# Front of a fused attention and squared-ReLU kernel: q of chunks 2 and 3 loaded ahead of the weights and multiplied while chunks 0 and 1 are normalised

## The chip, the cores and the metric

The kernel runs on one core of a Trainium2 chip. The core has five engines with an instruction queue each: PE (TensorE, matrix products into PSUM), DVE (VectorE, elementwise work), ACT (ScalarE, activations, copies and scalings), POOL (GpSimd) and SP (SyncE, which here only issues transfers). ACT and POOL issue transfers too. The metric is device time in microseconds (us); of the kernel before there are three runs, of 921.12, 923.35 and 923.43 us, with a median of 923.35.

## The reference

```python
kv  = einsum('bhsd,bhse->bhde', k, v)          # 8 batches, 8 heads, 576 rows, 64 columns
o   = einsum('bhsd,bhde->bhse', q, kv)
rms = sqrt(mean(o * o, axis=-1) + 1e-6)
x   = (o / rms * g_norm)                        # then (B,H,S,D) -> (B*S, H*D): 4608 x 512
h   = x @ w_in                                  # 512 -> 2048
g   = s * maximum(h, 0)**2 + b
out = g @ w_out                                 # 2048 -> 512
```

q, k, v and g_norm are float32. w_in and w_out come as float64 and are turned into float32 on the chip.

## The kernel before

The 4608 rows of x are cut into chunks of 128 rows, counted from 0; four chunks make a unit of 512 rows. Each unit goes through attention, then through the first matrix product with ReLU and squaring, then through the second. While PE multiplies one unit, the attention of the next is woven in. Only unit 0 has nothing in front of it: its four chunks, 0 to 3 (called 1 to 4 in the wording of the change), are worked off by a straight list of calls at the end of the kernel, from line 1272 on. Everything below is about this front.

The order is written out by hand. The kernel uses a manual schedule, so each engine gets its instructions in the order of the calls; the framework only adds the semaphore waits. A call such as `product` puts instructions on several engines at once, so moving it moves work in several queues.

Attention of a chunk `c` has these steps (`attention`, line 414):

- `turn` (L431): four PE transposes of q into a PSUM bank.
- `take` (L436 on DVE, L438 on ACT): copy of the turned q to SBUF (tile `qT`).
- `product`: the product with the block-diagonal kv matrices (`bd_kv`) into a PSUM bank, then the square on ACT (L456) and the sum of squares on DVE (L458). Chunks 0 and 1 use four 128x128 matmuls (L91), chunks 2 and 3 sixteen that are 32 wide (L447).
- `norm`: root on ACT (L462), reciprocal and scaling on DVE (L464, L466) into the tile `xn`.
- `turn_x`: the turn of `xn` into `xT`. Chunks 0 and 1 go through PE (L484), and ACT copies them out of PSUM scaled by g_norm (L486). Chunks 2 and 3 are transposed by DVE (L490), and ACT scales them in place for both at once (`scale_x`, L501).

The weights come in tiles of 1 MB, as pairs of 32-bit words, into a ring of three raw buffers (`w_raw`). `send_w` issues the next load on SP. A tile is made float32 by four calls: `hi` (L225) and `lo` (L230) on ACT prepare the upper and lower word, `shift` (L235) and `plus` (L245) on DVE put them together; `plus` also sends the next load. Each may be called for half a tile. Tile 0 is `wa` of step 0, tile 1 is `wb` of step 0, tile 2 is `wa` of step 1, and so on.

The first product of unit 0 is cut into 16 slots (`mm1_plain`, line 660). Each multiplies one weight tile with 256 rows, in 8 matmuls (the trace records each as two, so as 16), and puts its ReLU on ACT (L673) and its squaring on DVE (L674) at the place where the slot is called:

- slot 0: tile 0 with chunks 0 and 1, into an `x` bank
- slot 1: tile 1 with chunks 0 and 1, into a `y` bank
- slot 2: tile 0 with chunks 2 and 3
- slot 3: tile 1 with chunks 2 and 3; slots 4 to 15 go on with tiles 2 to 7.

Within a slot the matmuls run over four quarters of the 512 columns of x, so the second half of a weight tile is needed only after half of them.

The transfers of the front are issued on two queues, SP and ACT. A transfer waits for an earlier one to land when it takes over its semaphore. In the list, q of chunks 0 and 1 is loaded first, then weight tile 0, then q of 2 and 3, then tiles 1 and 2. `warm(n)` puts n matmuls of no use (2n in the trace) in the queue, which keep PE busy.

Of the kernel before, what the change touches and what calls it, by code (L numbers as in the profile page):

```python
# [16 lines left out]
def kernel(  # L17
# [113 lines left out]
    def load_q(c, queues=(nc.sync, nc.sync), rest_on=nc.gpsimd):  # L131

        t = qp.tile([P, 2 * DM], FP32, name="q_sb", tag="q")
        q_tile[c] = t
        pieces = []
        for i in range(2):
            if c + i < R:
                q_in[c + i] = t[:, i * DM : i * DM + DM].rearrange("p (h d) -> p h d", h=H)  # L140
        for s, queue in enumerate(queues):
            for i in range(2):
                if c + i < R:
                    b, j, _ = parts(c + i)[s]
                    queue.dma_start(
                        out=q_in[c + i][s * HB : s * HB + HB],
                        in_=q[b].rearrange("h (p j) d -> p j h d", j=R)[:, j],
                    )
        for i in range(2):
            if c + i < R:  # L150
                continue
            w = 4 * i
            for b, j, n in parts(c + i):
                if pieces and pieces[-1][1] == b and pieces[-1][2] + pieces[-1][3] == j:
                    pieces[-1][3] += n
                else:
                    pieces.append([w, b, j, n])
                w += n
            q_in[c + i] = t.rearrange("p (a w) -> p a w", a=NP)[:, :, i * P : i * P + P]
            if c + i == R:  # L160
                q_in[R] = t[:, DM:].rearrange("p (a w) -> p a w", a=NP)
        rest = []
        for w, b, j, n in pieces:
            src = q[b].rearrange("h (t j) d -> h t j d", j=JC)
            to = t.rearrange("p (a w d) -> p a w d", a=NP, d=32)
            if c < R:
                to, w = t[:, DM:].rearrange("p (a w d) -> p a w d", a=NP, d=32), 0
            for h in range(H):
                for a in range(2):
                    rows = slice(32 * (2 * (h % 2) + a), 32 * (2 * (h % 2) + a) + 32)  # L170
                    rest.append(
                        partial(
                            rest_on.dma_start,
                            out=to[rows, h // 2, w : w + n, :],
                            in_=src[h, :, j : j + n, a * 32 : a * 32 + 32],
                        )
                    )
        return rest
# [183 lines left out]
    def warm(n):  # L362

        ps = ps_f.tile([P, 2, TB], FP32, name="warm_ps", tag="z", bufs=1)
        for _ in range(n):
            matmul(ps[:, 0, :P], ident, ident, True, True)
# [35 lines left out]
    def half_of(name, c):  # L402

        if c % 2 == 0:
            two_of[name] = attp.tile([P, 2 * DM], FP32, name=name, tag=name)
        t = two_of[name]
        if name == "qT":
            return t.rearrange("p (a x) -> p a x", a=NP)[:, :, c % 2 * P : c % 2 * P + P]
        return t[:, c % 2 * DM : c % 2 * DM + DM].rearrange("p (h d) -> p h d", h=H)

    def small(name, n, i=""):
        return attp.tile([P, n], FP32, name=name, tag=f"{name}{i}")

    def attention(c):

        st = {}  # L420

        def turn():
            st["qT"] = half_of("qT", c)
            if c in (0, 2):
                ps = ps_a.tile([P, NP, P], FP32, name="qT_ps", tag="x")
            elif c == 3:
                ps = bank_of("q", "z", 1).rearrange("p b (m n) -> p (b m) n", m=2)
            else:
                ps = ps_t.tile([P, NP, P], FP32, name="qT_ps", tag="t")
            for p in range(NP):  # L430
                nc.tensor.transpose(ps[:, p, :], q_in[c][:, 2 * p : 2 * p + 2, :], ident)  # L431
            st["q_ps"] = ps

        def take():
            if c != 1:
                nc.vector.tensor_copy(out=st["qT"], in_=st["q_ps"])  # L436
            else:
                nc.scalar.copy(st["qT"], st["q_ps"])  # L438

        def product():  # L440
            ps = bank_of("att", "xy"[c % 2]).rearrange("p b (m n) -> p (b m) n", m=2)
            if c < 2:
                for p in range(NP):
                    matmul(ps[:, p, :], st["qT"][:, p, :], bd_kv[0][:, p, :], True, True)
            for w in range(4 if c >= 2 else 0):
                for p in range(NP):
                    nc.tensor.matmul(  # L447
                        ps[32 * p : 32 * p + 32, w, :],
                        lhsT=st["qT"][:, p, 32 * w : 32 * w + 32],
                        rhs=bd_kv[0][:, p, :],  # L450
                        start=True,
                        stop=True,
                    )
            st["x"] = ps.rearrange("p c (l d) -> p (c l) d", l=2)
            st["xn"] = half_of("xn", c)
            nc.scalar.activation(st["xn"], st["x"], AF.Square)  # L456
            st["ss"] = small("ss", H, c % 2)
            nc.vector.reduce_sum(st["ss"], st["xn"], axis=mybir.AxisListType.X)  # L458

        def norm():  # L460
            rms = small("rms", H, c % 2)
            nc.scalar.activation(rms, st["ss"], AF.Sqrt, bias=eps_col, scale=1.0 / D)  # L462
            inv = small("inv", H, c % 2)
            nc.vector.reciprocal(inv, rms)  # L464
            shape = (P, H, KC, D // KC)
            nc.vector.tensor_tensor(  # L466
                out=st["xn"].rearrange("p h d -> p (h d)").rearrange(
                    "p (c h e) -> p h c e", c=KC, h=H
                ),
                in0=st["x"].rearrange("p h (c e) -> p h c e", c=KC),  # L470
                in1=inv.unsqueeze(2).unsqueeze(3).to_broadcast(shape),
                op=ALU.mult,
            )

        def turn_x():
            u, j = divmod(c, 4)
            if j == 0:
                xT[u] = xp.tile([P, KC, 2 * TB], FP32, name="xT", tag="xT")
            to = xT[u][:, :, j * P : j * P + P]
            if c < 2:  # L480
                ps = ps_t.tile([P, KC, P], FP32, name="xT_ps", tag="t")
                xn = st["xn"].rearrange("p h d -> p (h d)")
                for i in range(KC):
                    nc.tensor.transpose(ps[:, i, :], xn[:, i * P : i * P + P], ident)  # L484
                for i in range(KC):
                    nc.scalar.activation(  # L486
                        to[:, i], ps[:, i], AF.Copy, scale=g_col[:, i : i + 1]
                    )
                return
            nc.vector.transpose(  # L490
                out=to, in_=st["xn"].rearrange("p h d -> p (h d)").rearrange("p (c x) -> p c x", c=KC)
            )
            if j % 2 == 1:
                scale_x(u, j - 1)

        return turn, product, norm, turn_x, take

    def scale_x(u, j):
        to = xT[u][:, :, j * P : j * P + 2 * P]
# [136 lines left out]
    def bank_of(key, tag, bufs=2):  # L636
        bank[key] = ps_f.tile([P, 2, TB], FP32, name=f"{tag}_ps", tag=tag, bufs=bufs)
        return bank[key]
# [598 lines left out]
    def send_w():  # L1237
        if sent[0] < len(blocks):
            load_w(blocks[sent[0]])
            sent[0] += 1  # L1240
# [9 lines left out]
    def hi(n, h=None):  # L1250
        fold_hi(blocks[n], h)

    def lo(n, h=None):
        round_lo(blocks[n], h)

    def shift(n, h=None):
        shift_hi(blocks[n], place(n), h)
# [16 lines left out]
    for i in range(2):  # L1274
        load_kv(0, i, kv0p, two, tag="kv")
    load_q(0, two)
    send_w()
    load_q(2, two[::-1])
    for _ in range(2):
        send_w()  # L1280
    kv_product(0)
    kv0p.release()
    gp = ctx.enter_context(tc.tile_pool(name="gp", bufs=NS // 2))


    turn, product, norm, turn_x, take = zip(*(attention(c) for c in range(4)))
    slots0 = [slot for s in range(NS) for slot in mm1_plain(s)]
    turn[0]()
    turn[1]()
# [1 line left out]
    take[1]()  # L1291
    product[0]()
    product[1]()
    warm(7)
    norm[0]()
    hi(0, 0)
    norm[1]()
    shift(0, 0)
    hi(0, 1)
    lo(0, 0)  # L1300
    plus(0, 0)
    turn_x[0]()
    turn_x[1]()
    turn[2]()
    turn[3]()
    lo(0, 1)
    take[2]()
    take[3]()
    shift(0, 1)
    product[2]()  # L1310
    plus(0, 1)
    hi(1)
    product[3]()
    shift(1)
    lo(1)
    plus(1)
    norm[2]()
    turn_x[2]()
    norm[3]()
    turn_x[3]()  # L1320
    slots0[0]()
    slots0[1]()
    for step in (hi, lo, shift, plus):
        step(2)
# [212 lines left out]
```

## Time and profile before

The profiled execution has a span of 920.1 us. Busy times of the engines in it:

| engine | busy us | share of the span |
|---|---|---|
| PE | 908.6 | 99% |
| PE weight loads | 825.9 | 90% |
| DVE | 678.3 | 74% |
| ACT | 209.3 | 23% |
| POOL | 220.2 | 24% |

Over the first 50 us the busy times, the share of the DMA engines and the rate are:

| stretch (us) | PE | DVE | ACT | DMA share | GB/s |
|---|---|---|---|---|---|
| 0 to 10 | 7.36 | 0.22 | 1.28 | 0.77 | 186 |
| 10 to 20 | 8.16 | 3.02 | 2.49 | 1.13 | 292 |
| 20 to 30 | 7.73 | 7.65 | 8.13 | 0.62 | 203 |
| 30 to 40 | 9.73 | 6.87 | 6.57 | 0.55 | 188 |
| 40 to 50 | 10.00 | 7.53 | 6.04 | 0.85 | 283 |

A share of busy time is an average over a stretch. A matmul counts as busy from its start to a modelled end, so a busy PE need not be a PE at its peak; an idle PE is really idle. In a line of a timeline or a group, "L91" is the line of the kernel, "x_ps<-xT,wa" the tile written and the tiles read, "x16" the count, and what stands in square brackets or after the second bar is idle time of the engine ahead of it and what ended it.

### The profile page before, as it was taken

How to read it: one execution, taken by the hardware profiler on the slowest of the kernel's cores; microseconds unless marked ns; L12 is line 12 of the kernel's file. 1: busy time of each engine (PE TensorE's matmuls, PEld its weight loads, DVE VectorE, ACT ScalarE, POOL GpSimd, SP SyncE). 2: the span in 40 equal slices, each digit the busy share in tenths (PEclk: the TensorE clock that was granted, in tenths of full speed). 3: DMA queues.
4: the chain of work that ended last, by engine and by line, in shares of the span. 5: the costliest groups of instructions: out<-in, count | busy, mean ns of one | idle time of the engine just before them, and what ended most of it. 6: DMA issues, size and time to landing. Idle time of an engine off the chain costs nothing.

```text
span 920.1 us, 18318 instructions
## 1 busy us (share of the span) xinstructions
PE 908.6 (99%) x7286; PEld 825.9 (90%) x7286; DVE 678.3 (74%) x1144; ACT 209.3 (23%) x383; POOL 220.2 (24%) x412
## 2 busy tenths in 40 slices
PE   7999999999999999999999999999999999999998
PEld 6888888888889998899889988999899988998898
DVE  2779778687577986887677867787678768864685
ACT  2674122211124003310232013301330033002200
POOL 2000016112613232721274025603430300020000
PEclk9999999999999999999999999999999999999999
DMA  9587937339922994189426954497428800890085
GB/s 254 189 302 253 280 98 229 103 86 346 324 81 51 279 325 115 22 244 309 149 54 173 303 163 114 109 295 234 117 54 289 279 9 12 266 307 24 12 252 184
DMA packets 113605, 167.70 MB, mean 182 GB/s; under 512 B 28400, under 2 KB 45552, under 8 KB 113520
## 3 DMA queue, kind: packets, MB, share of 16 engines
q1 hardware_dynamic: 95504, 141.98, 49.5%
q0 software_dynamic: 14560, 22.31, 8.7%
q10 hardware_dynamic: 3456, 2.23, 1.0%
q8 instruction: 58, 0.95, 0.4%
q14 instruction: 27, 0.22, 0.1%
HBM read 142.35 MB, written 24.12 MB: 181 GB/s over the span
## 4 chain that ended last, share of the span: by engine, by line
PE 95%; DMA 2%; DVE 1%; ACT 1%; issue 0%; SPq 0%; ACTq 0%; DVEq 0%
PE x_ps L91 51%; PE y_ps L91 29%; PE z_ps L91 11%; PE y_ps L550 2%; PE kv_ps L380 2%; DMA w_raw<-in_moe_w_in_dram 1%; DMA kv_sb<-in_k_dram 1%; ACT w_raw L230 0%; PE qT_ps L539 0%; DVE o L849 0%; ACT w_raw L225 0%; DVE xT L490 0%; DVE xn L466 0%; SPq L107 0%; DVE sub L253 0%
## 5 line engine op out<-in xcount | busy, mean ns | idle before, releaser
L1357 POOL DMA_DIRECT2D q_sb<-in_q_dram x256 | 143.6, 569 | 150.0 <-issue 118.8
L694 ACT COPY r<-x_ps 128x512 f32<-128x512 f32 x96 | 55.9, 583 | 453.4 <-PE x_ps L91 423.6
L958 POOL DMA_DIRECT2D out_dram<-o x110 | 54.8, 505 | 403.5 <-DVE o L849 277.1
L91 PE MATMUL x_ps<-w_sb,sub 128*128 128x128 f32 x1176 | 149.3, 276 | 0.7 <-DVE r L849 0.7
L91 PEld LDWEIGHTS x_ps<-w_sb,sub 128*128 128x128 f32 x1176 | 139.7, 192 | 1.5 <-DVE r L849 0.9
L91 PE MATMUL x_ps<-xs,ws 128*128 128x256 f32 x512 | 122.3, 382 | 0.0
L91 PE MATMUL y_ps<-xs,wb 128*128 128x256 f32 x512 | 121.7, 380 | 0.0
L91 PEld LDWEIGHTS x_ps<-xs,ws 128*128 128x128 f32 x512 | 96.2, 190 | 16.5 <-issue 3.8
L91 PEld LDWEIGHTS y_ps<-xs,wb 128*128 128x128 f32 x512 | 96.7, 190 | 13.8 <-DVE s L250 0.4
L250 DVE TENSOR_TENSOR a<-y_ps,r 128x512 f32<-128x512 f32 x64 | 44.1, 689 | 82.9 <-ACT r L694 73.1
L91 PE MATMUL x_ps<-xT,wa 128*128 128x256 f32 x384 | 89.6, 380 | 0.1
L91 PEld LDWEIGHTS x_ps<-xT,wa 128*128 128x128 f32 x384 | 72.3, 190 | 10.2 <-ACT xT L501 0.5
L91 PE MATMUL x_ps<-w_sb,a 128*128 128x128 f32 (+1 forms) x432 | 64.9, 298 | 0.0
L91 PE MATMUL y_ps<-w_sb,a 128*128 128x128 f32 (+1 forms) x416 | 62.1, 295 | 0.0
L91 PEld LDWEIGHTS x_ps<-w_sb,a 128*128 128x128 f32 x432 | 59.0, 191 | 3.2 <-issue 0.4
L91 PE MATMUL x_ps<-xT,ws 128*128 128x256 f32 x256 | 61.2, 382 | 0.0
L91 PE MATMUL z_ps<-xT,wa 128*128 128x256 f32 x256 | 60.5, 379 | 0.0
L649 DVE SCALAR_TENSOR_TENSOR a<-a 128x512 f32<-128x512 f32 x82 | 56.7, 692 | 2.8
L91 PEld LDWEIGHTS y_ps<-w_sb,a 128*128 128x128 f32 x416 | 56.1, 192 | 2.1
L91 PEld LDWEIGHTS z_ps<-xT,wa 128*128 128x128 f32 x256 | 48.6, 190 | 6.6
L91 PEld LDWEIGHTS x_ps<-xT,ws 128*128 128x128 f32 x256 | 48.1, 190 | 6.5
L849 DVE SCALAR_TENSOR_TENSOR r<-x_ps,s_col,o 128x256 f32<-128x256 f32 (+1 forms) x84 | 34.8, 414 | 25.7 <-PE x_ps L91 23.9
(154 smaller groups left out, 1264.7 us busy)
## 6 DMA issues: line engine op xcount, KB each, us to landing
w_sb<-w SPq DMA_DIRECT2D x343, 256.0 KB, 4.8
w_raw<-in_moe_w_in_dram SPq DMA_DIRECT2D x8, 1024.0 KB, 9.0
w_raw<-in_moe_w_out_dram SPq DMA_DIRECT2D x8, 1024.0 KB, 5.2
w_sb<-w SPq DMA_DIRECT2D x14, 512.0 KB, 8.5
w<-sub POOLq DMA_DIRECT2D x28, 256.0 KB, 6.4
w_sb<-in_k_dram SPq DMA_DIRECT2D x24, 288.0 KB, 4.7
w_sb<-in_v_dram SPq DMA_DIRECT2D x24, 288.0 KB, 5.0
out_dram<-o POOLq DMA_DIRECT2D x92, 64.0 KB, 3.8
```

The lines of the kernel that those rows point to most:

```text
L91: nc.tensor.matmul(o, lhsT=lhsT, rhs=rhs, start=start, stop=stop, skip_group_check=True)
L250: nc.vector.tensor_tensor(out=o, in0=a, in1=b, op=ALU.add)
L380: nc.tensor.matmul(ps[r][(r ^ l) * HB : (r ^ l) * HB + HB, i, :], lhsT=kv[l][0][rows, j, :], rhs=kv[l][1][rows, j, :], start=(j == 0), sto ...
L550: nc.tensor.matmul(ps[l][32 * p : 32 * p + 32, r, lo:hi], lhsT=bd_kv[b % 2][rows, p, at : at + 32], rhs=st["qT"][rows, p, lo:hi], start=Tr ...
L649: nc.vector.scalar_tensor_tensor(t, t, 0.0, t, ALU.max, ALU.mult)
L694: nc.scalar.copy(st[name], src)
L849: nc.vector.scalar_tensor_tensor(o, ps, s_col, other, ALU.mult, ALU.add)
L958: queues[s % 2].dma_start(out=view[b, jj, :, cols], in_=st[name, j][s * w : s * w + w, cols])
L1357: load()
```

## The change

The change rearranges the front, in five parts:

1. q of chunks 2 and 3 is loaded ahead of weight tile 0.
2. Chunks 2 and 3 are turned, taken and multiplied while chunks 0 and 1 are being normalised. The banks of the turns and the engines of the copies are dealt out anew for this: even chunks go through the `x` bank and DVE, odd ones through a `y` or `z` bank and ACT. The `warm(7)` between goes away.
3. `product` and `norm` are split, so that squares and roots have calls of their own; the roots of 0 and 1 stand ahead of the weight conversions. Squares of 2 and 3 come later than before relative to their products.
4. Tile 1 is converted in two halves, and slot 0 is called ahead of them, directly after tile 0's second half. Slot 1 stays at the end.
5. `turn_x` of chunk 1 is scaled on DVE in place of ACT.

Its purpose is to let slot 0 start earlier, without the turns and products of chunks 2 and 3 in its way.

```diff
         def turn():
-            if c in (0, 2):
+            if c % 2 == 0:
                 ps = ps_a.tile([P, NP, P], FP32, name="qT_ps", tag="x")
-            elif c == 3:
-                ps = bank_of("q", "z", 1).rearrange("p b (m n) -> p (b m) n", m=2)
             else:
-                ps = ps_t.tile([P, NP, P], FP32, name="qT_ps", tag="t")
+                tag, bufs = ("y", 2) if c == 1 else ("z", 1)
+                ps = bank_of("q", tag, bufs).rearrange("p b (m n) -> p (b m) n", m=2)
...
         def take():
-            if c != 1:
+            if c % 2 == 0:
...
             st["x"] = ps.rearrange("p c (l d) -> p (c l) d", l=2)
+
+        def square():
             st["xn"] = half_of("xn", c)
...
+        def root():
+            st["rms"] = small("rms", H, c % 2)
+            nc.scalar.activation(st["rms"], st["ss"], AF.Sqrt, bias=eps_col, scale=1.0 / D)
+
         def norm():
-            rms = small("rms", H, c % 2)
-            nc.scalar.activation(rms, st["ss"], AF.Sqrt, bias=eps_col, scale=1.0 / D)
...
-                    nc.scalar.activation(
-                        to[:, i], ps[:, i], AF.Copy, scale=g_col[:, i : i + 1]
-                    )
+                    if c == 0:
+                        nc.scalar.activation(
+                            to[:, i], ps[:, i], AF.Copy, scale=g_col[:, i : i + 1]
+                        )
+                    else:
+                        nc.vector.tensor_scalar(
+                            out=to[:, i], in0=ps[:, i], scalar1=g_col[:, i : i + 1],
+                            scalar2=None, op0=ALU.mult,
+                        )
...
     load_q(0, two)
-    send_w()
-    load_q(2, two[::-1])
-    for _ in range(2):
+    load_q(2, two)
+    for _ in range(3):
         send_w()
...
     product[1]()
-    warm(7)
-    norm[0]()
-    hi(0, 0)
-    norm[1]()
-    shift(0, 0)
-    hi(0, 1)
-    lo(0, 0)
-    plus(0, 0)
-    turn_x[0]()
-    turn_x[1]()
+    square[0]()
+    square[1]()
     turn[2]()
     turn[3]()
+    root[0]()
+    norm[0]()
+    root[1]()
+    take[2]()
+    norm[1]()
+    take[3]()
+    hi(0, 0)
+    product[2]()
+    lo(0, 0)
+    shift(0, 0)
+    turn_x[0]()
+    plus(0, 0)
+    product[3]()
+    hi(0, 1)
+    turn_x[1]()
     lo(0, 1)
-    take[2]()
-    take[3]()
     shift(0, 1)
-    product[2]()
     plus(0, 1)
-    hi(1)
-    product[3]()
-    shift(1)
-    lo(1)
-    plus(1)
+    slots0[0]()
+    square[2]()
+    hi(1, 0)
+    lo(1, 0)
+    shift(1, 0)
+    plus(1, 0)
+    square[3]()
+    hi(1, 1)
+    lo(1, 1)
+    shift(1, 1)
+    plus(1, 1)
+    root[2]()
     norm[2]()
     turn_x[2]()
+    root[3]()
     norm[3]()
     turn_x[3]()
-    slots0[0]()
     slots0[1]()
```

More of the change, by code (lines that the diff above doesn't have):

```diff
@@ L458, in product @@
             nc.vector.reduce_sum(st["ss"], st["xn"], axis=mybir.AxisListType.X)
+        def root():
+            st["rms"] = small("rms", H, c % 2)
+            nc.scalar.activation(st["rms"], st["ss"], AF.Sqrt, bias=eps_col, scale=1.0 / D)
         def norm():
-            rms = small("rms", H, c % 2)
-            nc.scalar.activation(rms, st["ss"], AF.Sqrt, bias=eps_col, scale=1.0 / D)
             inv = small("inv", H, c % 2)
-            nc.vector.reciprocal(inv, rms)
+            nc.vector.reciprocal(inv, st["rms"])
             shape = (P, H, KC, D // KC)
@@ L494, in turn_x @@
                 scale_x(u, j - 1)
-        return turn, product, norm, turn_x, take
+        return turn, take, product, square, root, norm, turn_x
     def scale_x(u, j):
@@ L1276 @@
     load_q(0, two)
-    send_w()
-    load_q(2, two[::-1])
-    for _ in range(2):
+    load_q(2, two)
+    for _ in range(3):
         send_w()
+    turn, take, product, square, root, norm, turn_x = zip(*(attention(c) for c in range(4)))
     kv_product(0)
@@ L1283 @@
     gp = ctx.enter_context(tc.tile_pool(name="gp", bufs=NS // 2))
-    turn, product, norm, turn_x, take = zip(*(attention(c) for c in range(4)))
     slots0 = [slot for s in range(NS) for slot in mm1_plain(s)]
```

## The prediction

> **What bounds the kernel now.** I read the chain of work that ended last first, by engine, to see who sets the end:
>
> ```profile
> PE 95%; DMA 2%; DVE 1%; ACT 1%; issue 0%; SPq 0%; ACTq 0%; DVEq 0%
> ```
>
> TensorE (PE) is nearly the whole chain. Then the busy times by stretch (columns: PE, weight loads, DVE, ACT, POOL, clock, share of the DMA engines, GB/s):
>
> ```profile
> 26.00:34.00 8.00, 7.46 (x37) 5.92 (x33) 6.75 (x11) 3.43 (x7) 0.00 (x0) 1.00 0.66 203
> 34.00:913.00 879.00, 878.34 (x6915) 799.14 (x6916) 662.58 (x1112) 196.85 (x356) 213.52 (x394) 1.00 0.59 181
> ```
>
> From 34 to 913 us the PE idles 879.00 - 878.34 = 0.66 us. The matmuls there are not edited, so the end moves by as much as the start of that unbroken stretch moves. Which matmul starts it? The timeline of PE (start, length, what):
>
> ```profile
> 26.01 3.72 PE L91 MATMUL x_ps<-xT,wa 128*128 128x256 f32 x16
> 30.17 3.72 PE L91 MATMUL y_ps<-xT,wb 128*128 128x256 f32 x16 [0.44 <-DVE wb L245]
> 33.99 3.72 PE L91 MATMUL x_ps<-xT,wa 128*128 128x256 f32 x16
> ```
>
> These are slots 0, 1 and 2. Slots 0 and 1 take chunks 0 and 1 with the weight tiles wa and wb; slot 2 takes chunks 2 and 3. **Slot 2 at 33.99 is the number to predict.** The chain in order of time (start, length, what) shows what it waited for:
>
> ```profile
> 28.89 1.23 DVE wb L245
> 30.12 0.12 DVE inv L464
> ...
> 30.33 0.70 DVE xn L466
> ...
> 31.06 0.71 DVE xT L490
> ...
> 31.96 0.70 DVE xn L466
> ...
> 32.69 0.72 DVE xT L490
> ...
> 33.43 0.52 ACT xT L501
> ...
> 33.99 3.72 PE x_ps L91 x16
> ```
>
> DVE finishes wb at 30.12, then normalises and transposes chunks 2 and 3. That tail is 33.99 - 30.12 = 3.87 us, and the change leaves it as it is. Last, where ACT runs the ReLUs (L673) of slots 0 and 1:
>
> ```profile
> 33.43 1.70 ACT L501 ACTIVATE xT<-xT,g_col 128x256 f32<-128x256 f32 x4 [4.57 <-DVE xT L490]
> 35.04 0.57 ACT L673 ACTIVATE a<-x_ps 128x512 f32<-128x512 f32 x1
> 35.52 0.58 ACT L673 ACTIVATE a<-y_ps 128x512 f32<-128x512 f32 x1
> ```
>
> Slot 0's matmuls end at 26.01 + 3.72 = 29.73, its ReLU runs at 35.04. ACT has no work waiting on slot 0 before chunks 2 and 3 are finished. This place in the order is what the change moves.
>
> [...] ACT's next weight conversion starts at 35.99, right behind the two ReLUs and with no wait for a transfer of its own.
> [...] the clock reads 1.00 throughout.
> [...]
>
> **The change part by part.** Prices come from the groups by form:
>
> ```profile
> L225 ACT ACTIVATE w_raw<-w_raw 128x512 f32<-128x512 f32 x2 | 1.3, 656 | 1.3 <-DMA w_raw<-in_moe_w_in_dram 1.3
> L230 ACT ACTIVATE w_raw<-w_raw 128x512 uint32<-128x512 uint32 x2 | 1.4, 696 | 0.0
> L235 DVE TENSOR_SCALAR wa<-w_raw 128x512 uint32<-128x512 uint32 x2 | 0.8, 419 | 0.0
> L245 DVE CUSTOM_DVE_ANT_0 wa<-w_raw,wa 128x1024 uint16<-128x1024 uint16 x2 | 1.4, 687 | 0.1
> L458 DVE TENSOR_REDUCE ss<-xn 128x8 f32<-128x512 f32 x4 | 2.7, 686 | 3.3 <-ACT xn L456 3.3
> ```
>
> *Transfers.* q of chunks 2 and 3 (4 x 128 KB = 0.52 MB) goes ahead of the first weight tile, whose conversion could start at 20.22 (the chain). Served strictly in turn the tile lands 0.52 MB / 292 GB/s (the rate of 10 to 20 us) = 1.8 us later, at 22.0. At the other end: by 20 us 1.86 + 2.92 = 4.78 MB had moved, while k, v (2.36), all q (1.05) and one tile (1.05) are 4.46 MB, so the bytes alone allow 19.1. I take 21, between these.
>
> *Chunks 0 and 1, start of slot 0.* Up to the sum of squares of chunk 1 (DVE free at 19.51) little changes: chunk 1's turn now uses a bank of its own, but the products still wait for DVE's copy of chunk 0 at 15.98. The 7 warm matmuls go, and the turns of 2 and 3 take their place. DVE then runs: norm of 0 to 20.42, copy of 2 (0.69) to 21.1, norm of 1 (0.2 + 0.69) to 22.1. PE: product of 2 (1.08) from 21.1, turn of xn 0, product of 3, turn of xn 1, each pair about 1.3, ending near 24.0. DVE scales chunk 1 (4 new instructions; bounds 0.17 by the 128x128 memset and 0.29 by the 64x128 copy out of PSUM at L394[...]), the first at 24.3. The first weight half is ready at 21 + 0.66 + 0.70 + 0.69 = 23.1, or 24.1 if the tile lands at 22; so PE's and DVE's chain sets the start, and the late tile is hidden by it. The second half is ready near 26.2, when half of the slot's matmuls (half of 3.72) have run: no wait. **Slot 0 starts at 24.3 and ends at 28.0, 1.7 us ahead of before.**
>
> *Slot 0's ReLU.* It is now queued on ACT ahead of the squares of 2 and 3 and of both halves of the second weight tile, and its squaring on DVE ahead of their sums, shifts and adds. None of these starts before slot 0 ends, ready or not. After the end DVE has, in order: wait for the ReLU 0.04 + 0.57; squaring 0.69; sum of 2 0.69; shift 0.42; add 0.69; sum of 3 0.69; shift 0.42; add 0.69. That is 4.90, and with some 0.03 at each of seven handovers 5.1. ACT's seven instructions beside it overlap (starts 0.5 apart, as 20.25, 21.01 with a root between, 21.55) and end near 3.8, before the last add at 4.4. Slot 1 can start after the first add: 0.61 + 0.69 + 0.69 + 0.42 + 0.69 + 0.1 = 3.2 us in which PE is idle; before it was 0.44. So slot 1 runs from 31.2 to 34.9.
>
> *Slot 2.* 28.0 + 5.1 + the unchanged tail 3.87 = **37.0, against 33.99: 3.0 us later**, with PE idle another 2.1 us ahead of it. Roots ahead of conversions and halves of the second tile shorten waits within these chains, and are in the sums; half operations cost 1.10 on DVE for each half against 0.69 + 1.23 for a whole, 0.3 us more in all. Later tiles are converted after slot 1's ReLU, as before, with two slots in between; so nothing is gained back or lost there.
>
> 923.35 + 3.0 = **926.4 us**.
>
> **The rivals.**
> 1. *The early half runs better* (925.4). Slot 0 starts when the first weights are ready at 23.3, because PE and DVE work off the turns sooner; slot 2 at 36.0, + 2.0. For: the handovers are my assumption. Against: DVE's queue up to 22.1 is summed from measured durations.
> 2. *It costs more* (927.7). The tile lands after 23 [...], or the 3.2 us gap brings the clock down and slot 1 takes up to twice 3.72, ending at 38.4 in place of 34.9: slot 2 is then 38.4, + 4.4. [...] Against: [...] 2.1 us of the loss is hidden.
> 3. *The head start carries through* (921.7, on the other side): slot 0 is 1.7 us earlier and slots 1 and 2 follow without a gap. For: q of chunks 2 and 3 is multiplied early, off slot 0's path. Against: the ReLU's place in both queues; even without it the DVE items of the list (3.6) and the tail (3.87) from 26.2 give 33.7, only 0.3 better.
>
> **How the numbers follow.** Forecast 0.55, rival 1 0.20, rival 2 0.18, rival 3 0.07. The range runs from one microsecond under rival 1 (the times before spread over 2.3 us) to 0.7 over rival 2: 924.4 to 928.4; it leaves out rival 3 and tails. 0.3% is 2.8 us, so the forecast lies barely over it: three quarters of its 0.55 and all of rival 2 give slower 0.59; the rest of it and rival 1 give same 0.34; faster 0.07.
>
> **What would show it.** In the profile after: slot 0 at about 24.3; slot 0's ReLU starting as its matmuls end, with ACT idle before it; PE idle some 3 us ahead of the first y_ps slot, put down to DVE's add (L245); slot 2 near 37.0; no PE idle later. I am wrong if slot 1 follows slot 0 within 1 us, if slot 2 starts before 35, or if PE waits later than slot 2.

## The result and the profile after

The changed kernel takes 926.91 us (median of 6 runs, 926.31 to 928.29), against 922.99 us for the kernel before (6 runs, 921.12 to 923.51). The ratio is 1.0050 with a 95% interval of 1.0036 to 1.0064: slower by 3.9 us in the medians. The profiled execution has a span of 924.5 us against 920.1; it is the fastest of the six. Line numbers of the changed kernel are shifted by up to 9: the ReLU of the slots is L682, their squaring L683, the square of the attention L457, its sum L459, the scaling of the turned chunks L490 (on ACT), L494 (on DVE) and L510.

PE is still the chain of work that ended last:

```profile
PE 97%; DVE 1%; DMA 1%; issue 0%; SPq 0%; ACT 0%; DVEq 0%
```

The busy times by stretch (PE, weight loads, DVE, ACT, POOL, clock, share of the DMA engines, GB/s) show where the loss lies:

```profile
26.00:34.00 8.00, 4.74 (x17) 3.46 (x16) 4.98 (x10) 4.16 (x9) 0.00 (x0) 0.79 0.45 132
30.00:38.00 8.00, 6.36 (x16) 5.12 (x17) 5.98 (x12) 4.15 (x11) 0.00 (x0) 0.57 0.55 188
34.00:913.00 879.00, 878.12 (x6888) 797.86 (x6887) 660.41 (x1107) 197.15 (x356) 213.52 (x394) 1.00 0.58 181
```

From 26 to 34 us PE is busy for 4.74 us where it had been 7.46. From 34 to 913 us it is busy as before, to 0.2 us, though its first 4 us are now slot 1 at a low clock (0.56 on average from 34 to 38 us). The clock, 1.00 over the same stretches before, is 0.57 on average from 30 to 38 us. The timeline of PE has slots 0, 1 and 2 again:

```profile
24.54 3.84 PE L91 MATMUL x_ps<-xT,wa 128*128 128x256 f32 x16 [0.54 <-DVE xT L494]
31.64 6.58 PE L91 MATMUL y_ps<-xT,wb 128*128 128x256 f32 x16 [3.26 <-DVE wb L245]
38.06 3.62 PE L91 MATMUL x_ps<-xT,wa 128*128 128x256 f32 x16
```

Slot 0 starts 1.5 us earlier than before. Then PE waits 3.26 us for DVE, slot 1 runs for 6.58 us in place of 3.72, and slot 2 starts at 38.06 in place of 33.99: 4.07 us late, of the 4.4 by which the spans differ. The chain in order of time between slots 0 and 1:

```profile
24.54 3.85 PE x_ps L91 x16
...
28.41 0.60 ACT a L682
...
29.04 0.52 DVE a L683
...
29.65 0.68 DVE ss L459
30.33 0.34 DVE wb L235
...
30.80 0.70 DVE wb L245
...
31.64 6.58 PE y_ps L91 x16
```

Slot 0 itself, its ReLU and its squaring are on it, ahead of a sum of chunk 2 and of weights that need nothing from slot 0. ACT's timeline shows the hold:

```profile
28.41 0.60 ACT L682 ACTIVATE a<-x_ps 128x512 f32<-128x512 f32 x1 [3.74 <-PE x_ps L91]
28.91 0.59 ACT L457 ACTIVATE xn<-x_ps 128x512 f32<-128x512 f32 x1
29.38 0.67 ACT L225 ACTIVATE w_raw<-w_raw 128x512 f32<-128x512 f32 x1
```

ACT idles 3.74 us for slot 0's last matmul. Product 2, which the square (L457) reads, had been in PSUM since 21.8. The conversion of tile 1 (the last line) doesn't wait for its transfer either: it was issued at 13.69 and took 10.3 us, so the tile was there at 24.0, before slot 0 began. The last add of tile 1 on DVE, and ACT's scaling of chunks 2 and 3, which slot 2 needs:

```profile
32.56 0.69 DVE L245 CUSTOM_DVE_ANT_0 wb<-w_raw,wb 128x1024 uint16<-128x1024 uint16 x1
36.42 1.70 ACT L510 ACTIVATE xT<-xT,g_col 128x256 f32<-128x256 f32 x4 [3.85 <-DVE xT L499]
```

### The profile page after: what moved, and what is told of

It is laid out like the page before. It is cut to its first block, busy times and chain, and to the rows that moved or that the text cites. A ratio compares the mean times of both kernels' runs of the same rounds, so it can differ in the third digit from the quotient of the medians.

```text
span 924.5 us, 18300 instructions
## 1 busy us (share of the span) xinstructions
PE 911.0 (99%) x7272; PEld 827.1 (89%) x7272; DVE 678.8 (73%) x1149; ACT 209.2 (23%) x382; POOL 220.2 (24%) x412
## 4 chain that ended last, share of the span: by engine, by line
PE 97%; DVE 1%; DMA 1%; issue 0%; SPq 0%; ACT 0%; DVEq 0%
PE x_ps L91 51%; PE y_ps L91 29%; PE z_ps L91 11%; PE kv_ps L380 2%; PE y_ps L559 2%; DMA kv_sb<-in_v_dram 1%; PE qT_ps L548 0%; SPq L107 0%; DVE o L858 0%; DVE ss L459 0%; DVE sub L253 0%; DVE qT L435 0%; DVE xn L592 0%; DVE a L253 0%; PE xT_ps L487 0%
```

## The experiments

The theory: slot 0's ReLU and squaring, called early, hold ACT's and DVE's work behind them until slot 0 ends (in the changed kernel's trace the two idle for 3.74 and 2.71 us), and in the PE gap that this makes the clock falls too (to 0.50 there from 31 to 32 us). The rivals: the new load order, or the dropped fill matmuls, cost the time. A time is the median; the ratio is to runs of the kernel before on the same chip. The medians of the kernel before were 922.41, 923.55 and 922.73 us in the three groups of runs (e1 to e4, e5 to e8, e9 to e11), each group on another chip. Every run also has its mean clock over the whole execution. In e1's trace, where the clock averages 0.58 from 22 to 26 us and 1.00 over the 4 us on either side, it reads 0.998, in traces without such a stretch 1.000 (e2, e5, e9 to e11) or 0.999 (e6 and e8, whose slots 1 and 2 take 3.68 to 3.72 us); so 0.998 and below is called a low mean clock here.

**e1: slot 0's ReLU and squaring back at the end.** PE's queue stays in the order of the changed kernel, as slot 0 and slot 1 have no PE work between them; only ACT's and DVE's queues change.

```diff
     plus(0, 1)
-    slots0[0]()
     square[2]()
...
     turn_x[3]()
+    slots0[0]()
     slots0[1]()
```

> The changed kernel with only the call of slot 0 moved back to the end of the list, directly ahead of slot 1. Theory (slot 0's ReLU and squaring hold ACT's and DVE's queues until slot 0 ends): the 3.3 us idle of PE between slots 0 and 1 goes, slot 1 follows at about 28.2, no clock drop; slot 2 is then set by DVE's own work (second half of tile 0 ready 26.3, then sums, shifts and adds 3.6, tail 3.87) at about 33.8, so about 922.7 us, 4 below the changed kernel and no more than 0.5 below the kernel before. Rival (the loss is in the new load order, or in the dropped fill matmuls): it stays at 926 to 927.

923.43 us (921.64 to 925.00), ratio 1.0005 (0.9998 to 1.0011). PE's timeline has slots 0, 1 and 2:

```profile
26.29 3.84 PE L91 MATMUL x_ps<-xT,wa 128*128 128x256 f32 x16 [0.54 <-DVE xT L494]
29.99 3.69 PE L91 MATMUL y_ps<-xT,wb 128*128 128x256 f32 x16
35.34 3.72 PE L91 MATMUL x_ps<-xT,wa 128*128 128x256 f32 x16 [1.66 <-ACT xT L510]
```

The gap behind slot 0 is gone and the loss with it, so the rivals fall as the main cause. (The ReLU and the squaring moved together, so how much of the loss each of the two queues alone would make isn't separated.) But the profiled run, at 924.52 us one of the slowest, started slot 2 at 35.34, not 33.8. The stretches say why:

```profile
18.00:22.00 4.00, 1.96 (x42) 1.52 (x40) 3.65 (x8) 2.80 (x6) 0.00 (x0) 1.00 1.03 370
22.00:26.00 4.00, 3.76 (x44) 2.71 (x40) 0.96 (x3) 2.40 (x7) 0.00 (x0) 0.58 0.62 232
```

PE was busy for only half of 18 to 22 us (its longest wait there is 2.04 us, for the copy of chunk 2), and then its clock fell to 0.58: product 3 took 1.94 us in place of 1.08, and slot 0 started at 26.29. The changed kernel has the same 2.0 us wait, yet its profiled run kept 1.00 from 22 to 26 us. So this drop comes in some runs and not in others. The mean clocks of e1's 21 runs agree: ten are low, and these take 923.05 to 925.00 us; the eleven others take 921.64 to 923.56.

**e6 and e11: the same with 8 fill matmuls in that wait** (twice, as the measure for two groups).

```diff
     turn[3]()
+    warm_t(8)      # as warm(8), into a bank of the turns
     root[0]()
```

> The version with slot 0 called late, plus 8 fill matmuls on PE in its own 2.0 us wait for the copy of chunk 2 (behind the turn of chunk 3). Theory (what kept the late version at 923.4 is the clock falling in that wait in some of its runs, which stretched product and turns and moved slot 0 from 24.5 to 26.3): no run with a dropped clock in the front, slot 2 at about 33.7, median 921.7 to 922.2, and a spread under 2 us. Rival (spread and median come from elsewhere, as transfers): median and spread as without the fill, 923.4, 3.4 us.

> The late version with 8 fill matmuls once more, as the measure for the two runs beside it on the same chip: 921.9, slot 2 9.0 us after the start of slot 0.

921.87 us (921.58 to 923.05), ratio 0.9983 (0.9975 to 0.9992), slot 2 at 34.00; and 922.08 us, ratio 0.9992 (0.9984 to 1.0000), slot 2 at 34.15. None of these 27 runs has a low mean clock, against ten of 21 in e1; of the runs of the kernel before beside them, 14 of 25 and 11 of 27 have one. The spread falls from 3.4 us to 1.5 and 1.4. PE's timeline of e6:

```profile
24.96 3.84 PE L91 MATMUL x_ps<-xT,wa 128*128 128x256 f32 x16 [0.54 <-DVE xT L500]
28.64 3.68 PE L91 MATMUL y_ps<-xT,wb 128*128 128x256 f32 x16
34.00 3.72 PE L91 MATMUL x_ps<-xT,wa 128*128 128x256 f32 x16 [1.68 <-ACT xT L516]
```

In both traces slot 2 starts 9.04 us after slot 0, and it stands where it stood before the change (33.99): the early turns and products bring slot 2 no earlier by themselves. That e6 is below the kernel before in time goes with the low clock in more than half of the runs beside it.

**e2: fill in the gap behind slot 0**, to take the clock out of the loss.

```diff
     slots0[0]()
+    warm(12)
     square[2]()
```

> The changed kernel with 12 fill matmuls queued on PE directly behind slot 0 (about 2.8 us of the 3.3 us gap). Theory (part of the loss is the clock, which falls to half in the gap so that slot 1 takes 6.6 us): slot 1 takes 3.7 us again and slot 2 starts when its rows are scaled, at about 36.95 in place of 38.06: about 925.8 us, 1.1 below the changed kernel. If the clock isn't caused by the gap: 926.9, slot 1 still at 6.6 us. In no theory does it reach the kernel before.

925.56 us, ratio 1.0042 (1.0029 to 1.0056). PE's timeline, with the fill and slots 1 and 2:

```profile
28.69 2.84 PE L91 MATMUL warm_ps<-ident 128*128 128x128 f32 x24
32.03 3.75 PE L91 MATMUL y_ps<-xT,wb 128*128 128x256 f32 x16 [0.49 <-DVE wb L245]
37.47 3.72 PE L91 MATMUL x_ps<-xT,wa 128*128 128x256 f32 x16 [1.69 <-ACT xT L510]
```

Slot 1 is back at 3.75 us, and slot 2 waits for its rows, not for slot 1. It starts 12.45 us after slot 0 (25.02); in the changed kernel it was 38.06 - 24.54 = 13.52. So the clock costs 1.1 us in the trace. The intervals of the two ratios overlap, so the times alone don't separate it. Two of the five runs have a low mean clock all the same (926.87 and 927.53 us), as the wait for chunk 2 isn't filled here; the three others take 925.19 to 925.56.

**e3: the kernel before with slot 0 called early**, load order and fills as before.

```diff
     plus(0, 1)
+    slots0[0]()
     hi(1)
...
     turn_x[3]()
-    slots0[0]()
     slots0[1]()
```

> The kernel before with one call moved: slot 0 directly behind the add of the second half of weight tile 0, ahead of the conversion of tile 1; load order, fills and steps of attention as before. Theory (queue place): slot 0 starts near 25.1 and ends near 29, its ReLU then holds the conversion of tile 1, slot 1 starts near 34 after an idle PE of 4 us or more, slot 2 at 37.8, or at up to 40.6 if the clock drops: 926.8 to 929.6 us. Rival (load order or dropped fill): no change, 923.

927.00 us, ratio 1.0056 (1.0044 to 1.0069). In the trace, of a run of 928.54 us, slot 1 starts after a PE wait of 3.88 us (the window ends within slot 2):

```profile
34.79 6.19 PE L91 MATMUL y_ps<-xT,wb 128*128 128x256 f32 x16 [3.88 <-DVE wb L245]
40.81 2.54 PE L91 MATMUL x_ps<-xT,wa 128*128 128x256 f32 x11
```

One moved call makes a loss as large as the change's in a kernel that has none of the other parts. It isn't as clean as e1, because here slot 0 also stands ahead of product 3 on PE, which runs at 29.83 in place of 25.02.

**e4: the kernel before with the new load order alone.**

```diff
     load_q(0, two)
-    send_w()
-    load_q(2, two[::-1])
-    for _ in range(2):
+    load_q(2, two)
+    for _ in range(3):
         send_w()
```

> The kernel before with only the new load order: q of chunks 2 and 3 ahead of weight tile 0. Theory: the weights land no later than before (19.9 against 20.2 in the two traces), and the start of slot 2 hardly moves: 922.5 to 923. Rival (late weights cost): tile 0 lands 1 to 2 us later, slot 2 as much later: 924 to 925.

923.24 us, ratio 1.0008 (1.0000 to 1.0016): 0 to 1.5 us slower, so more than I expected and less than the rival. In its trace, and then in the changed kernel's, which has the same order, the first conversion of tile 0 reads:

```profile
21.30 0.65 ACT L225 ACTIVATE w_raw<-w_raw 128x512 f32<-128x512 f32 x1 [2.12 <-DMA w_raw<-in_moe_w_in_dram]
```

```profile
19.88 0.66 ACT L225 ACTIVATE w_raw<-w_raw 128x512 f32<-128x512 f32 x1
```

The tile is there 1.5 us later in e4's trace: issued at 13.68 it takes 7.6 us, in the changed kernel's issued at 13.07 it takes 6.7. That trace is of the slowest of the 14 runs and has a low clock too (0.70 from 22 to 26 us), as have seven of the 14 (nine of 34 of the kernel before beside them). So this part is small and not pinned down. In the changed kernel the conversion doesn't wait for the tile.

**e9: slot 0 called between the halves of tile 1** (with e6's fill), which puts half the work behind its ReLU.

> The late version with 8 fill matmuls, but slot 0 called between the two halves of tile 1: its ReLU and squaring hold only the second half's work. Theory (the cost is what stands behind the ReLU in the queues, item by item): after slot 0's end DVE has squaring, sum of 3, shift, add and the tail, about 3.1 + 3.87, so slot 2 starts 10.8 after the start of slot 0 in place of 9.0: 1.8 us above the late version with the same fill, about 923.6. Rival (all or nothing, only the position ahead of the whole tile matters): as the late version, 921.9.

923.70 us, ratio 1.0009 (1.0001 to 1.0017), 1.6 us above e11 beside it. The two halves of slot 1, and slot 2:

```profile
28.28 1.92 PE L91 MATMUL y_ps<-xT,wb 128*128 128x256 f32 x8
31.62 1.99 PE L91 MATMUL y_ps<-xT,wb 128*128 128x256 f32 x8 [1.41 <-DVE wb L245]
35.30 3.72 PE L91 MATMUL x_ps<-xT,wa 128*128 128x256 f32 x16 [1.68 <-ACT xT L516]
```

Slot 2 starts 35.30 - 24.61 = 10.69 us after slot 0, between 9.04 (late) and 12.45 (early). At these three places the cost follows what stands behind the ReLU.

**e10: the changed kernel with both fills.**

> The changed kernel (slot 0 called early) with both fills, 8 matmuls in the wait for chunk 2 and 12 behind slot 0: the price of the queue place without any dropped clock. Theory: slot 2 starts 12.4 after the start of slot 0 in place of 9.0: 3.4 us above the late version with the fill, about 925.3, with the clock at 1.00 in the front.

927.71 us, ratio 1.0052 (1.0039 to 1.0065): 2.4 us over what I expected, and 5.6 above e11 beside it where 3.4 was expected. The front is as expected: slot 2 at 37.51, 12.45 us after slot 0, clock 1.00. The waits of PE in the stretch from 100 to 120 us hold something new:

```profile
PE x_ps L91 <- issue: 1.4, 1, 1.4
```

PE stood for 1.4 us with nothing that the profile shows to wait for. It isn't in the trace of e2, whose slot 2 starts at the same time. Why it comes here, and where the last microsecond went, stays open. Five of the six runs have a mean clock of 0.999 or 1.000, and still they take as long as the changed kernel's. So the split of the loss, 3.4 us for the queue place and 1.1 for the clock, rests on the traces and on e2 and is not confirmed by this time.

**e5 and e7: a version to beat both.** From e1: the copy of chunk 2 on ACT, right behind the root of chunk 0; the squares written over q, so that they need not wait for xn to be turned; chunk 2's square ahead of the copy of the turned chunk 0. e7 adds `warm(6)` behind slot 1.

```diff
         def take():
-            if c % 2 == 0:
+            if c == 0:
...
-            nc.scalar.activation(st["xn"], st["x"], AF.Square)
+            nc.scalar.activation(q_in[c], st["x"], AF.Square)
...
     root[0]()
-    norm[0]()
-    root[1]()
     take[2]()
+    norm[0]()
+    root[1]()
...
     plus(0, 0)
+    square[2]()
+    turn_x[0]()
     product[3]()
```

> Slot 0 called late, and besides: the copy of chunk 2 on ACT instead of DVE, the squares of all chunks written over q in place of xn, so that they need not wait for the turn of xn, and the square of chunk 2 ahead of the copy of the turned chunk 0. Theory (slot 2 is set by DVE's list of work; product 2 starts at 19.3 instead of 20.7 and DVE loses 0.7 us and some idle time): slot 0 near 22.8, slot 2 near 31.5, so about 920.3 us, 2 below the kernel before. Rival (transfers or PE set slot 2): 922 to 923.

> The same as the version with the copy of chunk 2 on ACT, plus 6 fill matmuls behind slot 1, in PE's wait for slot 2 (about 1.5 us of some 1.9). Theory: if the clock falls in that wait in some runs, this one is 0.5 us or more below the other in the median; if it doesn't, the two are the same at 920.3.

920.30 us (920.20 to 920.80), ratio 0.9964 (0.9952 to 0.9977), and 920.37 us, ratio 0.9965 (0.9953 to 0.9978). Fill behind slot 1 makes no difference. PE's timeline of e5:

```profile
23.77 3.84 PE L91 MATMUL x_ps<-xT,wa 128*128 128x256 f32 x16 [0.72 <-DVE xT L494]
27.45 3.62 PE L91 MATMUL y_ps<-xT,wb 128*128 128x256 f32 x16
32.22 3.72 PE L91 MATMUL x_ps<-xT,wa 128*128 128x256 f32 x16 [1.16 <-ACT xT L510]
```

Slot 0 is 1.0 us later than I reckoned and slot 2 0.7, still 1.8 us ahead of the kernel before. DVE now works from 19.7 to 31.6 us almost without a pause, so its list of work is probably what is left to shorten. The PE wait of 2.04 us is down to 0.48, none of the ten runs has a low mean clock, and they spread over 0.6 us (e5) and 1.2 (e7). Against e6 beside it e5 gains 1.6 us. Its three edits weren't run one by one.

**e8: the kernel before with `warm(4)` between its turns of xn.**

> The kernel before with 4 fill matmuls between the two turns of xn, where its PE waits about 1.1 us for ACT. Theory (the kernel before has runs with a dropped clock in its front too, which make its spread of 3.5 us): median lower by 0.3 to 0.8 us, 921.6 to 922.1, and fewer runs above 923. Rival: no difference, or 0.5 slower because the fill delays a turn.

922.46 us, ratio 0.9992 (0.9983 to 1.0000): the right way, but on the edge of what can be measured. The clock is clearer: none of the 13 runs has a low mean clock, against 14 of the 25 of the kernel before beside them. Yet runs with a mean clock of 1.000 still go up to 924.17 us, so the clock isn't the only source of the spread.

## Why the prediction was right, by its steps

- **Slot 2 is the number to predict: held.** Span less start of slot 2 is 886.1 us before, 886.4 after, 886.1 in e6 and 886.2 in e5. Where it is larger (887.5 in e4, 887.4 in e1, 887.0 in e9, 886.8 in e11), PE waits a second time near the bias row, 1.2, 0.7, 0.6 and 0.4 us, put down to DVE; e10 (887.9) has the wait of 1.4 us. The start itself was forecast at 37.0 and came at 38.06, for the clock (below).
- **Transfers: tile at 21, wrong by 1.2 us, and without effect.** It was there at 19.8 and its conversion ran at 19.88 without a wait. As the prediction said, the PE and DVE chain sets the start. (By the prediction's own numbers the lower bound is 18.9, not 19.1.)
- **Slot 0 at 24.3: 24.54.** The turns of xn end at 24.01, as forecast, but by two errors that cancel: product 2 starts at 20.74 (21.1), and a product with its turn takes 1.6 us in the chain (1.3). The scaling was an estimate, 0.3 us in the step from 24.0 to 24.3, and its upper bound, 0.29, is too low: in the trace one takes 0.345 us, and four take 1.13. Slot 0 waits for the whole of the first, and 0.36 us of it and 0.14 to the matmul stand in the chain; this is why slot 0 is 0.24 us late.
- **The ReLU's place: held.** PE waits 3.26 us (3.2 predicted). DVE's list ends at 32.56 + 0.69 = 33.25, so 4.86 us after slot 0's end at 28.39 (5.1 predicted); ACT's ends 3.8 after it, as predicted. The tail is 3.69 us (3.87). Slot 2's rows are ready at 36.42 + 0.52 = 36.94 (0.52 as in the chain before), where the forecast had 37.0. That this is so close is in part luck: slot 0 ends 0.4 us later than forecast, and the list and the tail are 0.4 shorter.
- **The clock: I gave this to rival 2, and it came.** Slot 1 took 6.58 us, so slot 2 started 1.1 us after its rows were ready. The rival had up to twice 3.72 and slot 2 at 38.4; it started at 38.06. (Twice 3.72 from 31.2 gives 38.6; the prediction's 38.4 is a slip.) So the measured case is the forecast's chain plus most of that rival's clock: +3.9 us where the forecast had +3.0. The time itself is only 0.5 us above the forecast because the prediction started from 923.35, while the kernel before has 922.99 over six runs. I also counted on a gap of 3.2 us being too short to lower the clock, which no trace had shown, and that was wrong: behind a gap of 3.26 us slot 1 ran at a clock of 0.50 up to 37 us, and the clock had fallen at most 2.6 us after slot 0's last matmul (0.84 from 30 to 31 us, 0.50 from 31 to 32; slot 0 ends at 28.4). The mean clock is low (0.994 to 0.996) in all six runs. That the clock read 1.00 throughout before is right up to 913 us; from 913 us to the end, where PE is busy for 3.28 of 7.05 us, it reads 0.96. The argument against the rival, that 2.1 us of a slower slot 1 is hidden, held in kind: slot 1 took 2.9 us more and cost 1.1.
- **Rival 3's counter: held.** Even without the ReLU's hold slot 2 was to come at 33.7; e6 has 34.00 and e11 34.15. A head start for slot 0 isn't one for slot 2.

## What to carry to other kernels

A call that puts work on several engines puts it ahead of everything called later, on each of them: the early call of slot 0 kept ACT idle for 3.74 us with ready work behind it, DVE for 2.71, and PE then for 3.26. So place the part that waits for a long matmul group (here the ReLU and its squaring) behind the work that is ready, even when its matmuls should go first. Then find the start from which the bound engine runs without a break and move what that start waits for; in e6 slot 0 started 1.0 us earlier than in the kernel before and slot 2 did not, while e5, whose edits take work and waits off DVE, gained 1.6 us on e6. And look at the clock of every run: with 4 or 8 matmuls of no use in a PE wait of 1.1 us (e8) or 2.0 us (e6, e11) none of the 40 runs of these three has a low mean clock, where the same kernel without them has one in 14 of 25 runs (before, beside e8) and in ten of 21 (e1, on another chip).

## What the runs showed of the hardware that I had not expected

- PE's clock averaged 0.58 over the 4 us behind a stretch of 4 us in which PE was busy for 1.96 us, with no wait longer than 2.04 us (e1; in e4 0.70 after 2.54 busy us of 4). It came in some runs of a kernel and not in others: ten of 21 runs of e1 have a low mean clock. With eight fill matmuls in the wait none of 27 has one (e6, e11), and the spread of the times went from 3.4 us to 1.5 and 1.4, on other chips.
- In the changed kernel the clock had fallen to 0.50 by 31 us, after at most 2.6 us without a matmul.
- The first weight tile, sent in the same order, was there 6.7 us after its issue in one kernel's trace (the changed kernel) and after 7.6 us in another's (e4).
